# Attention with a learned position bias and a gated feed-forward block: bias stores moved from GpSimd's queue to SyncE's, one PSUM tile per half of a bias unit, and first attention steps placed between the last bias units

## The chip, the cores and the metric

The kernel runs on one core of a Trainium2 chip. The metric is the device time of one execution in microseconds (us); lower is better. The engines are TensorE (PE, its weight loads PEld), VectorE (DVE), ScalarE (ACT), GpSimd (POOL) and SyncE (SP), which issues most transfers. Each engine works through its own instructions in a fixed order.

## The reference, cut to what matters

Four batches, eight heads, 576 positions, head size 64. The bias added to the scores is a small two-layer network of the distance between two positions, divided by a factor of the row; it is the same for all batches. After the attention the eight heads are joined to 512 channels and a gated product of two linear layers (512 to 1536) goes through a third (1536 to 512).

```python
psi_rel = log1p(|i - j|);  psi_i = log1p(max(i, 1))
h = maximum((psi_rel / psi_i) * w1 + b1, 0)        # 32 hidden
scores = q @ k.T / 8 + (h @ w2)                    # bias per head
attn = softmax(scores) @ v                         # then heads joined: x
out = ((x @ w_a) * (x @ w_b)) @ w_out
```

## The kernel before, in words

**The bias.** The 576 rows are cut into units of 16. For the row chunk that is done first (rows 0 to 255) there are 16 units. A unit takes four hidden blocks of 128 partitions (`bias_relu`, L152: a scale and relu of a row of logarithms, on DVE at L160 or on ACT at L164; `nact` says how many go to ACT), four groups of matmuls with `w2` into PSUM (`bias_mm`, L168, L170), and one or two scaled copies from PSUM to an SBUF row `bo` on ACT (L186, and L189, which reads backwards and so mirrors the row). Units 0 to 3 are wider than 512 columns and are done in two halves; units 4 to 15 in one piece. A transfer then stores `bo` to the DRAM tensor `bias_d` (L191), from POOL's queue for these 16 units. In `first_units` the PSUM tile is `[128, 2, 512]`, one per unit, from two pools in turn (`two`, L923); both halves of a unit lie in one tile. `keep(n)` issues n matmuls on a block of ones whose result nobody reads (L897).

**The attention of the first batch.** `attn_steps` yields twice per tile of 128 rows; tile n needs its bias rows, loaded from `bias_d` on SP (`load_bias`, L480), its scores (`qk_pair`, L526, two heads at once), a sum with row minimum on DVE (`soft1`, L540), an exponential on ACT (L545), a normalisation (`soft2`, POOL and DVE, L590 to L596), a transpose on PE (`turn`, L608) with a copy on ACT, and the product with v (`pv_first`, L557). Tiles 0 to 7 need rows 0 to 127, so units 0 to 7 of the bias; tiles 8 to 15 need units 8 to 15.

**The feed-forward weights** come as 64-bit numbers in chunks of 512 KB (`w_load`, L275) and are converted on ACT and DVE (`w_unit`, L281 to L287, then `wab_parts`), one chunk per step of `wab_steps`. `fetch_to(3)` loads the first three chunks in its first step. `v_scale` (L226) takes the largest magnitude of v with four ACT passes (L237) and a small matmul.

**The order.** PE's order is the program's (`manual_schedule`); on the other engines a scheduler places the instructions, and `issue_after`, `paced` and `late` add orders: a load under `paced` stands behind the last entry of `rows_in` on SP's queue, work under `late` behind the last entries of `ttrs`, `exps`, `evs` and `pns` on its engine. In the head of the kernel (L926 to L940) `merge` interleaves generators: units 0 to 7 with the loads of q, k and v (`first_loads`), the first weight step, bias loads 0 to 5, then units 8 to 15 with `v_scale` and two weight steps, eight `keep` matmuls, and then the attention steps with weight steps between.

## Time and profile before

| | |
|---|---|
| median of three runs | 748.81 us |
| the runs | 749.63, 744.23, 748.81 us |
| the profiled execution | 744.93 us |
| its span | 743.1 us |
| PE, DVE, ACT, POOL busy | 94%, 68%, 59%, 39% |
| mean granted clock of TensorE | 0.988 |

The span reaches from the first to the last instruction; 1.8 us of the profiled execution lie outside it. A busy share is an average over stages: the change touches the first 40 us or so, where PE is far from full, and the rest has to be read as what follows from them.

### The profile page before, as it was taken

The numbers are of one execution on the slowest core, as the hardware profiler recorded it, in microseconds if no ns is written. First come the engines' busy times: TensorE is split into PE (matmuls) and PEld (weight loads), VectorE is DVE, ScalarE is ACT, GpSimd is POOL, SyncE is SP. The second block draws the span as 40 slices with busy tenths as digits, with TensorE's granted clock in tenths as the row PEclk, the third lists the DMA queues.
The fourth block names the chain that finished last, engine by engine and source line by source line (L and its number), as shares of the span: only waits on it lengthen the run. The fifth ranks groups of instructions, "written<-read, shape, count | busy, mean of one in ns | idle before, by whom it ended". The sixth has DMA issues, their size and how long they took to land.

```text
span 743.1 us, 15586 instructions
## 1 busy us (share of the span) xinstructions
PE 695.8 (94%) x5463; PEld 531.0 (71%) x5463; DVE 506.9 (68%) x1234; ACT 436.2 (59%) x957; POOL 291.0 (39%) x429
## 2 busy tenths in 40 slices
PE   6887899899899999999899799999999999999997
PEld 1255466688686565677687688888788888888886
DVE  7788799989964776666888879888987780211100
ACT  6867787878966687744565555565655653322310
POOL 3544423336762142333454335535553563311200
PEclk9999999999999999999899999999999999999999
DMA  8899776687744987999999999999999973000001
GB/s 249 298 390 305 239 238 215 203 286 247 239 135 129 226 214 145 211 207 199 272 224 260 242 265 252 235 239 259 244 275 249 223 132 112 2 10 21 1 15 43
DMA packets 178163, 147.69 MB, mean 199 GB/s; under 512 B 125092, under 2 KB 138148, under 8 KB 178084
## 3 DMA queue, kind: packets, MB, share of 16 engines
q1 hardware_dynamic: 170928, 130.92, 69.6%
q10 hardware_dynamic: 5876, 10.93, 5.2%
q0 software_dynamic: 1280, 4.84, 1.8%
q8 instruction: 43, 0.70, 0.4%
q14 instruction: 36, 0.29, 0.1%
HBM read 101.15 MB, written 17.18 MB: 159 GB/s over the span
## 4 chain that ended last, share of the span: by engine, by line
PE 52%; DVE 12%; issue 11%; POOL 9%; DMA 8%; ACT 6%; SPq 1%; POOLq 0%; ACTq 0%; DVEq 0%
PE ab L770 22%; PE o L814 15%; PE pv L636 5%; PE qk L512 4%; POOL ph L575 4%; PE psta L170 3%; DMA pt<-ph 3%; DVE p L540 2%; POOL sm L590 2%; POOL gl L790 2%; DMA wraw<-wb 2%; ACT p L545 2%; DMA bias<-bias_d 1%; DVE ks L417 1%; DVE ph L578 1%
## 5 line engine op out<-in xcount | busy, mean ns | idle before, releaser
L770 PEld LDWEIGHTS <-w16t 128*128 128x128 f16 x2592 | 248.2, 98 | 45.2 <-issue 13.1
L770 PE MATMUL ab<-x,w16t 128*128 128x256 f16 x2304 | 271.9, 274 | 0.9 <-DVE x L651 0.9
L545 ACT ACTIVATE p<-p,mn 128x576 f32<-128x576 f32 x144 | 111.7, 776 | 82.3 <-DVE mn L540 70.8
L578 DVE SCALAR_TENSOR_TENSOR ph<-p,sm,ph 128x64 f16<-128x64 f32 x192 | 108.5, 605 | 23.0 <-POOL ph L575 22.6
L540 DVE CUSTOM_DVE_ANT_0 p<-qk,bias 128x576 f32<-128x576 f32 x143 | 106.5, 747 | 24.9 <-PE qk L512 12.9
L814 PE MATMUL o<-wos,gh 128*128 128x512 f32 x384 | 120.3, 394 | 0.0
L575 POOL TENSOR_SCALAR ph<-p,sm 128x576 f16<-128x576 f32 x96 | 71.5, 745 | 118.5 <-DVE sm L591 111.2
L590 POOL TENSOR_SCALAR sm<-sm 128x1 f32<-128x1 f32 x144 | 58.3, 405 | 140.4 <-ACT p L545 138.8
L790 POOL TENSOR_TENSOR gl<-g,gh 128x256 fp32r<-128x256 f32 x96 | 72.7, 757 | 88.1 <-ACT gh L789 88.0
L754 DVE SCALAR_TENSOR_TENSOR g<-ab,wv,asb 128x256 f32<-128x256 f32 x84 | 40.3, 480 | 80.9 <-ACT asb L778 79.6
L789 ACT CAST gh<-g 128x256 fp32r<-128x256 f32 x96 | 38.8, 404 | 76.3 <-DVE g L754 76.2
L814 PEld LDWEIGHTS o<-wos,gh 128*128 128x128 f32 x384 | 69.5, 188 | 16.0 <-issue 3.7
L512 PE MATMUL qk<-ks,qs 128*128 128x288 f32 x384 | 73.6, 313 | 5.6 <-DVE mn L540 3.8
L814 PE MATMUL o<-wos,gl 128*128 128x512 f32 x192 | 75.0, 391 | 0.0
L512 PEld LDWEIGHTS qk<-ks,qs 128*128 128x128 f32 x384 | 56.3, 190 | 15.9 <-DVE mn L540 5.4
L596 POOL TENSOR_SCALAR p<-p,sm 128x576 f32<-128x576 f32 x48 | 48.0, 1000 | 31.4 <-DVE sm L591 25.9
L778 ACT ACTIVATE asb<-ab,wv 128x256 f32<-128x256 f32 x84 | 39.4, 469 | 28.9 <-PE ab L770 26.0
L636 PE MATMUL pv<-pt,vs 128*64 128x320 f16 (+1 forms) x560 | 43.2, 308 | 9.3 <-DMA pt<-ph 9.3
L636 PEld LDWEIGHTS <-vs 128*64 128x64 f16 x560 | 32.0, 114 | 21.9 <-issue 9.3
L608 PE MATMUL tp<-idn,p 128*128 128x128 f32 x240 | 36.6, 285 | 6.2 <-ACT ptf L613 6.2
L814 PEld LDWEIGHTS o<-wos,gl 128*128 128x128 f32 x192 | 36.0, 188 | 7.8
L821 ACT COPY osb<-o 128x512 f32<-128x512 f32 x18 | 10.5, 582 | 52.5 <-PE o L814 36.6
(105 smaller groups left out, 913.5 us busy)
## 6 DMA issues: line engine op xcount, KB each, us to landing
bias<-bias_d SPq DMA_DIRECT2D x127, 288.0 KB, 3.8
rv<-vd SPq DMA_DIRECT2D x32, 320.0 KB, 4.3
rk<-kd SPq DMA_DIRECT2D x24, 288.0 KB, 3.6
wraw<-wa SPq DMA_DIRECT2D x12, 512.0 KB, 6.6
wraw<-wb SPq DMA_DIRECT2D x12, 512.0 KB, 5.0
wraw<-wo SPq DMA_DIRECT2D x12, 512.0 KB, 4.1
bias_d<-bo ACTq DMA_DIRECT2D x20, 295.5 KB, 3.4
bias_d<-bo POOLq DMA_DIRECT2D x16, 295.5 KB, 7.6
```

Of the source, the lines that this page charges most:

```text
L512: nc.tensor.matmul(ps[:, hf, :HB], a, b[:, hf * HB:hf * HB + HB], start=(x == 0), stop=(x == len(prods) - 1))
L540: ttr = nc.vector.tensor_tensor_reduce(out=p.rearrange("p (a n) -> p a n", a=2), in0=ps[:, :, :HB], in1=bt.rearrange("p (a n) -> p a n", a=2),
L545: exps.append(nc.scalar.activation(p, p, AF.Exp, bias=mn, scale=-1.0, accum_out=sm))
L575: nc.gpsimd.tensor_scalar(out=ph[:, :S], in0=p, scalar1=rc, scalar2=1.0, op0=ALU.mult, op1=ALU.mult)
L578: ins = nc.vector.scalar_tensor_tensor(out=ph[:, o:o + c1 - c0], in0=p[:, c0:c1], scalar=rc, in1=ph[:, c0:c1], op0=ALU.mult, op1=ALU.subtract,
L590: nc.gpsimd.tensor_scalar(out=sm, in0=sm, scalar1=1e-9, scalar2=1.0 / (PS if u >= NF else 1.0), op0=ALU.add, op1=ALU.mult)
L596: nc.gpsimd.tensor_scalar(out=p, in0=p, scalar1=rc, scalar2=1.0, op0=ALU.mult, op1=ALU.mult)
L636: nc.tensor.matmul(ps[64 * j:64 * j + 64, o:o + N], v[:, j, :], p[:, j * N:j * N + N], start=(x == 0), stop=(x == len(prods) - 1),)
L754: nc.vector.scalar_tensor_tensor(out=g, in0=ab[:, 1], scalar=wv[:, f, 1:2], in1=asb, op0=ALU.mult, op1=ALU.mult)
L770: nc.tensor.matmul(ab[:, j], w16[nm, f][:, pw, kk, :], xs[px][:, kk, :], start=(x % (3 * KC) == 0), stop=(x % (3 * KC) == 3 * KC - 1),)
L790: nc.gpsimd.tensor_tensor(out=gl, in0=g, in1=gh.bitcast(F32), op=ALU.subtract)
L814: nc.tensor.matmul(o, g[:, sl], wos[f][:, p], start=(f == 0 and x == 0), stop=(f == FC - 1 and x == 2))
```

## The change

The stores of units 0 to 7 go on SP's queue, those of units 8 to 15 stay on POOL's. A store on SP is entered in `rows_in`, so that later paced loads stand behind it. All q and k loads are issued first, then units 0 to 7 with the first weight step (now two chunks) after unit 4, then bias loads 0 to 3, the v loads, and bias loads 4 and 5. Every half of a unit takes a PSUM tile of its own from a ring: four tiles for units 0 to 7, two (those that the attention's first scores don't use) for units 8 to 15. The last copy of a unit is entered in `evs`. Three attention steps stand between units 10 and 11, one between 13 and 14, and the copies of units 14 and 15 are ordered behind the last exponential. From unit 8 on, odd units have all four relus on DVE, and each unit has two `keep` matmuls; the block of eight is gone.

```diff
@@ bias_unit
-                nc.scalar.mul(ob[:, mid + c0:mid + e], ps[:, :e - c0], rl)
+                ev = nc.scalar.mul(ob[:, mid + c0:mid + e], ps[:, :e - c0], rl)
...
-        queue.dma_start(out=dst[:, :, :BW - 1], in_=ob[:, :BW - 1])
+        store = queue.dma_start(out=dst[:, :, :BW - 1], in_=ob[:, :BW - 1])
+        if queue is nc.sync:
+            rows_in.append(store)
+        return ev
@@ wab_steps
-        fetch_to(3)
+        fetch_to(2)
@@ first_units
-                hs = bias_relu(lambda g: h4[:, g], uls, un, int(un % 2 == 0 or un >= 8))
-                keep((10, 2, 2, 2, 1, 1, 1)[un] if un < 7 else 0)
-                bias_unit(bh, lambda: banks(un), un, hs, 6, nc.gpsimd)
+                hs = bias_relu(lambda g: h4[:, g], uls, un, int(un % 2 == 0))
+                keep((10, 2, 2, 2, 1, 1, 1)[un] if un < 7 else 2)
+                evs.append(bias_unit(bh, lambda: banks(un), un, hs, 6, nc.sync if un < NU0 // 2 else nc.gpsimd))
@@
-        def two(un):
-            return (qkp, eq)[un % 2].tile([128, 2, 512], F32, tag="qk", name="psta", bufs=1)
+        def banks(un):
+            ring = (0, 1, 2, 3) if un < NU0 // 2 else (2, 3)
+            i = ring[used[0] % len(ring)]
+            used[0] += 1
+            if i == 3:
+                return pvp.tile([128, 1, 512], F32, tag="pv", name="psta", bufs=1)
+            pool, tag = ((qkp, "qk"), (eq, "qk"), (tpp, "tp"))[i]
+            return pool.tile([128, 2, 512], F32, tag=tag, name="psta", bufs=1)[:, 0:1]
...
-            merge((units, NU0 // 2), (fl, 2 * NP))
-            next(wts)
-            for m in range(6):
+            for _ in range(NP):
+                next(fl)
+            for un in range(NU0 // 2):
+                next(units)
+                if un == 4:
+                    next(wts)
+            for m in range(4):
                 load_bias(m)
-            merge((units, NU0 // 2), (v_scale(0), 7), (wts, 2))
-        keep(8)
-        merge((asteps, 4), (wts, 1), ((keep(2) for _ in range(4)), 4))
-        merge((asteps, 2 * N0 - 10), (wts, 7))
+            run(fl)
+            for m in range(4, 6):
+                load_bias(m)
+            vs0 = v_scale(0)
+            merge((units, 3), (vs0, 5), (wts, 1))
+            for _ in range(3):
+                next(asteps)
+            merge((units, 3), (wts, 1))
+            next(asteps)
+            with tc.issue_after(exps[-1].ins):
+                run(units)
+        merge((asteps, 2), (wts, 1), ((keep(2) for _ in range(2)), 2))
+        next(vs0)
+        merge((asteps, 2), ((keep(2) for _ in range(2)), 2))
+        run(vs0)
+        merge((asteps, 2 * N0 - 14), (wts, 7))
```

## Rows read from the trace of the kernel before

**Rows 1.** The page: busy tenths of PE and DVE in 40 slices of the span.

```profile
PE   6887899899899999999899799999999999999997
...
DVE  7788799989964776666888879888987780211100
```

**Rows 2.** Windows: stretch, length; PE, PEld, DVE, ACT, POOL busy (count); clock, DMA, GB/s.

```profile
5.00:24.70 19.70, 13.66 (x114) 2.93 (x113) 17.45 (x46) 16.02 (x38) 8.19 (x7) 1.00 0.90 305
24.70:36.00 11.30, 9.45 (x77) 3.06 (x78) 6.41 (x23) 9.00 (x21) 6.86 (x9) 1.00 0.85 250
36.00:48.00 12.00, 9.05 (x51) 5.43 (x52) 9.11 (x24) 7.37 (x16) 5.20 (x10) 0.89 1.03 414
...
85.00:95.00 10.00, 8.60 (x64) 4.94 (x63) 5.77 (x19) 5.18 (x13) 2.89 (x5) 1.00 0.49 130
95.00:140.00 45.00, 42.23 (x343) 29.60 (x340) 44.34 (x113) 33.73 (x66) 14.47 (x21) 1.00 0.67 216
```

**Rows 3.** Timeline around the two halves of unit 0: start, us, engine, line, instruction.

```profile
5.62 1.54 PE L170 MATMUL psta<-w16t,w2s 128*32 128x288 f32 x8 [0.41 <-DVE w16t L160]
...
7.23 0.50 ACT L186 ACTIVATE bo<-psta,rls 128x288 f32<-128x288 f32 x1 [0.77 <-PE psta L170]
7.63 0.27 ACT L189 ACTIVATE bo<-psta,rls 128x15 f32<-128x15 f32 x1
...
7.94 0.16 PEld L170 LDWEIGHTS psta<-w16t,w2s 128*32 128x32 f32 x8 [1.32 <-ACT bo L189]
```

**Rows 4.** Groups by line, 4 to 24.7 us: busy us, mean ns, idle before, releaser.

```profile
L160 DVE TENSOR_SCALAR w16t<-u,lgs 128x560 f32<-128x560 f32 (+11 forms) x40 | 15.9, 472 | 2.2 <-PE psta L170 2.2
L170 PE MATMUL psta<-w16t,w2s 128*32 128x288 f32 (+8 forms) x104 | 11.3, 473 | 5.7 <-ACT bo L189 5.3 <-DVE w16t L160 0.4
...
L897 PE MATMUL pr<-w16t 128*128 128x512 f16 x14 | 4.8, 429 | 0.0
L237 ACT ACTIVATE junk<-rvf 128x640 f32<-128x640 f32 x4 | 2.9, 732 | 0.0
...
L170 PEld LDWEIGHTS psta<-w16t,w2s 128*32 128x32 f32 x104 | 2.3, 108 | 12.6 <-ACT bo L189 9.1 <-DVE w16t L160 2.3 <-issue 1.1
```

**Rows 5.** The same view, 24.7 to 36 us.

```profile
L170 PE MATMUL psta<-w16t,w2s 128*32 128x432 f32 (+6 forms) x56 | 6.0, 498 | 2.2 <-ACT bo L189 2.2
```

**Rows 6.** Timeline from the stores to the first attention tiles.

```profile
24.30 0.37 ACT L189 ACTIVATE bo<-psta,rls 128x127 f32<-128x127 f32 x1
...
24.97 0.99 POOL L191 DMA_DIRECT2D bias_d<-bo  x1 [0.59 <-ACT bo L189]
...
28.49 2.52 SPq L480 DMA_DIRECT2D bias<-bias_d  x5
...
35.99 0.76 DVE L540 CUSTOM_DVE_ANT_0 p<-qk,bias 128x576 f32<-128x576 f32 x1 [3.15 <-PE qk L526]
...
37.73 1.24 PE L526 MATMUL qk<-rkf,rqf 64*128 64x288 f32 x8
...
39.34 0.71 PE L608 MATMUL tp<-idn,p 128*128 128x128 f32 x5
```

**Rows 7.** Tile view of the store at 24.97 us: issue to landing.

```profile
DMA to landing us min/median/max: 3.4/3.4/3.4
```

**Rows 8.** DMA issues of the first 30 us: KB each, median us to landing.

```profile
bias_d<-bo POOLq DMA_DIRECT2D x11, 295.5 KB, 5.8
rvf<-vd SPq DMA_DIRECT2D x4, 320.0 KB, 5.1
...
bias<-bias_d SPq DMA_DIRECT2D x4, 288.0 KB, 7.1
wraw<-wa SPq DMA_DIRECT2D x2, 512.0 KB, 9.4
```

**Rows 9.** The page, DMA issues of the whole span: stores of the later units.

```profile
bias_d<-bo ACTq DMA_DIRECT2D x20, 295.5 KB, 3.4
```

**Rows 10.** Timeline: the chunk that the fourth weight step waits for.

```profile
43.34 0.67 ACT L281 ACTIVATE wt<-wraw 128x512 f32<-128x512 f32 x1 [0.59 <-DMA wraw<-wb]
```

More of the change, by code (lines that the diff above doesn't have):

```diff
@@ L185, in bias_unit @@
             if e > c0:
-                nc.scalar.mul(ob[:, mid + c0:mid + e], ps[:, :e - c0], rl)
+                ev = nc.scalar.mul(ob[:, mid + c0:mid + e], ps[:, :e - c0], rl)
             a, e = max(c0, 1), min(c1, mid + 1)
             if e > a:
-                nc.scalar.mul(ob[:, mid + 1 - e:mid + 1 - a], ps[:, a - c0:e - c0][:, ::-1], rl)
+                ev = nc.scalar.mul(ob[:, mid + 1 - e:mid + 1 - a], ps[:, a - c0:e - c0][:, ::-1], rl)
         dst = bias_d[:, un * UP:un * UP + 16 * RW].rearrange("h (r w) -> r h w", w=RW)
-        queue.dma_start(out=dst[:, :, :BW - 1], in_=ob[:, :BW - 1])
+        store = queue.dma_start(out=dst[:, :, :BW - 1], in_=ob[:, :BW - 1])
+        if queue is nc.sync:
+            rows_in.append(store)
+        return ev
     def bias_rows(h, i, n):
@@ L921, in first_loads @@
                 yield
-        def two(un):
-            return (qkp, eq)[un % 2].tile([128, 2, 512], F32, tag="qk", name="psta", bufs=1)
+        def banks(un):
[6 more added lines that the diff above has]
+            return pool.tile([128, 2, 512], F32, tag=tag, name="psta", bufs=1)[:, 0:1]
+        used = [0]
         fl = first_loads()
@@ L929, in attention_moe @@
         with tc.tile_pool(name="bh", bufs=1, side="right") as bh:
-            units = first_units(two)
-            merge((units, NU0 // 2), (fl, 2 * NP))
-            next(wts)
-            for m in range(6):
-                load_bias(m)
-            merge((units, NU0 // 2), (v_scale(0), 7), (wts, 2))
-        keep(8)
-        merge((asteps, 4), (wts, 1), ((keep(2) for _ in range(4)), 4))
-        merge((asteps, 2 * N0 - 10), (wts, 7))
+            units = first_units(banks)
+            for _ in range(NP):
[5 more added lines that the diff above has]
+            for m in range(4):
+                load_bias(m)
+            run(fl)
[14 more added lines that the diff above has]
+        merge((asteps, 2 * N0 - 14), (wts, 7))
         n0 = 2 * ends[0] - 2 * N0 + 6
```

## The prediction

> **What bounds the kernel now.** I read the page first. PE is at nine tenths or more in nearly all slices after the first eight, and DVE is nearly full in the first eight [rows 1]. So from about 150 us on PE sets the pace, and what comes before is a start-up in which no engine is always full. A saving in the first 40 us is worth what it moves forward the work behind it, and no more.
>
> The windows by stage came next [rows 2]. From 95 to 140 us DVE is busy 44.34 of 45 us: it converts weights and reduces scores, and that work is the same before and after. Ahead of it DVE has idle time: 2.25 us of 19.70 in the stage of the first eight units, 4.89 of 11.30 in the stage of the last eight, 2.89 of 12.00 in the stage of the first attention tiles, and 4.23 of 10.00 from 85 to 95 us. The change can only pay by taking some of the first three away, about 10 us together; the fourth lies behind it and I see nothing in the change that touches it. The DMA share is 1.03 with 414 GB/s from 36 to 48 us, so in that stage the transfers are full as well.
>
> Then I followed the start of the attention through the timeline. The copies of unit 7 start their last part at 24.30, its store leaves POOL at 24.97, five bias loads leave SP from 28.49, DVE reduces the first scores at 35.99, PE makes the second pair of scores at 37.73 and the first transpose at 39.34 [rows 6]. The bias loads go the moment that the last store has landed: it took 3.4 us [rows 7].
>
> Why is unit 7 finished only at 24.7? The timeline of unit 0 shows it: its second half goes into the other bank of the tile, and still its weight load stands until the mirrored copy of the first half (7.63 to 7.90) is done, at 7.94 [rows 3]. In all, PE's weight loads lost 9.1 us behind these copies up to 24.7, and the matmuls 5.3 us of it beyond the loads' cover [rows 4]; the last eight units lost 2.2 us more [rows 5]. PE, ACT and the copies take turns where they could overlap.
>
> **The first eight units.** With a tile for each half and four in the ring, PE need not wait for the copy just made. What is left on PE is its own work. The 104 matmuls to 24.7 us take 11.3 us; eight of them are unit 8's, some 1.0, which leaves 10.3. The fillers of units 1 to 7 are eleven at 0.30 (two take 0.6), 3.3 us; the ten in front run before the data is there [rows 4]. From 5.6 us, where the first bias matmul starts [rows 3], that is 19.2. DVE's 28 relus at 0.40 (15.9 by 40) take 11.2 us and end before 17 [rows 4], and ACT loses the four passes over v (2.9 us) out of this stage, so neither is later than PE. The copies of unit 7 add 0.9, as now from the end of its matmuls without a queue. Unit 7 is done at 20.1 instead of 24.7: 4.6 us earlier. The bound below is no gain, if ACT's order keeps the turns; the bound above is this sum, since PE's work is not shortened.
>
> **The stores on SP.** POOL's queue loses eight stores and SP's gains eight, behind twelve loads of q and k and around two weight chunks (1 MB). A store behind unit 4 waits on SP for that unit's copies, and so do the chunks behind it; these chunks are not used before the weight step among units 8 to 10, so nobody waits. The landing time on SP's queue is not shown for this stage. From below it is the 3.4 us of the stores that ACT issues later [rows 9] and of POOL's last [rows 7]; from above the 9.4 us of the chunks in the first 30 us, with POOL's median of 5.8 between [rows 8]. I take 4.5: v (1.28 MB) and one chunk are no longer in front, two chunks are. Then the bias loads leave at 20.2 + 4.5 = 24.7 instead of 28.49, 3.8 us earlier; by the two ends 4.9 earlier or 1.1 later.
>
> **From the bias loads to the second tiles.** The loads land in 7.1 us [rows 8], so the first scores are reduced at about 31.3 and 32.0, against 35.99 [rows 6], where they also waited 3.15 us for PE's scores; these now stand between units 10 and 11, done before the bias. PE's count to that point: units 8 to 13 are 1.0 plus five sevenths of 6.0 (5.3 in all) [rows 5], fillers 12 at 0.3 (3.6), one pair of scores 1.24, so 29.3 from 19.2; then it stands until DVE has read both tiles, makes the second pair from 32.1 to 33.3 (38.97 before, 5.6 earlier), then units 14 and 15 with their fillers (1.6 + 1.2), the next fillers, and the first transpose at about 36.7, 2.6 us before its 39.34. If the loads land in 5.1 us as those of v did [rows 8], PE is there 2 us sooner. So this point moves forward by 2.6 on PE and 5.6 on DVE, whose second pair of tiles is the next to start. Between the two I take 4.5, nearer to DVE, because DVE and not PE is short of time until 140 us and PE has 2.95 idle us from 36 to 48 to catch up [rows 2].
>
> **What the edits cost.** Four relus move from ACT to DVE, at most 0.47 each [rows 4], 1.9 us; they lie in the 4.89 us that DVE idles in the second half of the units [rows 2], and cost 1.9 if that idle time has been used up. The four passes over v (2.9 us, their read-outs apart) go from this early stage to the time after the v loads land; ACT is busy 9.00 of 11.30 there [rows 2], but loses four relus, so I take nothing, with 2 us as the upper end. The third and fourth chunk are now issued behind the bias loads, v and two more bias loads, near 28.5; they land in 9.4 us [rows 8] or more, at 38, and the third is wanted by ACT near 36. Before, the fourth came late instead: ACT stood 0.59 us for it at 43.34 [rows 10]. I take 0.5 us more than now, from -1 to +3. Sixteen fillers among the units replace eight behind them; they are counted above. The stores of units 8 to 15 stay on POOL, whose queue has eight fewer ahead. The entries in `evs` and `rows_in` issue nothing.
>
> The sum: 4.5 - 0.5 = 4.0 us. From 48 us on the order of work is unchanged, DVE is full from 95 to 140 us and PE afterwards, so nothing I see gives the gain back, and nothing adds to it. 744.93 - 4.0 = 740.9 us for the profiled execution, 0.54% less. That execution is 0.5% under the median of the three runs; on the median the same ratio gives 748.81 x 0.9946 = 744.8 us.
>
> **Rivals.**
>
> *Most of it is lost in SP's order.* The last three stores stand on one queue behind two weight chunks instead of on a queue of their own. At the 305 GB/s of this stage [rows 2] 1 MB is 3.4 us, and the second chunk is not through when store 7 is issued. If all of that is ahead of it, it lands after 7.9 us, the bias loads leave at 28.1, hardly before 28.49, and of the 4.0 us some 0.6 is left: 748.2. For it: the chunks took 9.4 us [rows 8]. Against it: some 4 us lie between the chunks' issue after unit 4 and the store of unit 7. The Trainium skill, "DMA: Bandwidth & Descriptors", section "Queues, rings and completion order", says that a DMA engine takes turns between queue rows packet by packet but uses up one row's ring in order; by that rule a store on POOL's row shared the engines with the loads and one on SP's row must wait for them, which speaks against this part of the change. No row here shows the order within a queue.
>
> *The transfers set the pace anyway.* From 36 to 48 us they are full [rows 2], and v comes later than now. If the tiles of that stage wait for bytes, an earlier start only waits longer: about 0, 748.8. Against it: DVE lost 2.89 us there and the named wait for a chunk is 0.59 [rows 10].
>
> *It pays twice.* If the bias loads land in 3.4 to 5 us and the third chunk comes in time, PE is at the first transpose 5 us sooner, and the 2.89 idle us of DVE from 36 to 48 go too: 8 to 9 us, 740.
>
> *Slower.* The passes over v stand in ACT's fixed order between the copies of units 8 to 10. Their loads stand on SP behind four bias loads (0.5 us each to issue), which stand behind store 7's landing. If it lands after 9.4 us, at 29.6, the bias loads leave until 31.6, v until 33.6, and v lands at 5.1 to 7.1 after that, near 40. ACT then holds the copies of units 9 to 15 and the first exponentials until 40, PE and POOL's stores stand with it, and the exponential of tile 1 is some 5 us later than now, with the next bias loads behind units 8 to 15 another 3: 748.8 + 8 = 757. It decides from about 34 us on: up to there v is earlier than the exponentials want ACT.
>
> **How the numbers follow.** The forecast, 2 to 7.5 us less, 0.53; little or nothing left (the first two rivals, 3 us less to 3 more) 0.20; twice, 0.19; slower 0.08. What this kernel's measurement can tell from no change is about 1%, 7.5 us: its three runs are 0.7% apart. Faster by more than that is the third case and the edge of the first, 0.22; slower is most of the last, 0.06; the rest 0.72. The range, 738.5 to 752, takes in the third case but for its edge and the second to its end.
>
> **What would show it.** Right: no weight load of a second half behind the copy of the first; unit 7's copies done near 20 us; its store landing in 3.4 to 6 us; the bias loads leaving near 25; the first reduction on DVE near 31; the full stretch of DVE that begins at 95 us starting 4 us earlier. Wrong: store 7 landing after 8 us; ACT standing for v or for the third chunk by several us; the same idle time of DVE in the first 48 us; or the lead there at 48 us and gone at 140.

## The result and the profile after

The change makes the kernel slower. Twenty runs of the kernel after have a median of 750.81 us (745.91 to 753.09), twenty of the kernel before on the same chip 745.14 us (739.01 to 749.63); the ratio is 1.0068, 95% interval 1.0044 to 1.0093. I had forecast 0.54% faster. The profiled execution after has a span of 749.7 us with a mean granted clock of 0.975, the one before 743.1 us with 0.988. In the kernel after, lines behind 190 or so stand three further down: the score reduction is L543, the passes over v are L240, the fillers L900.

The page first, the tenths of PE and DVE over the span, against [rows 1].

```profile
PE   9688899899899999999898999999999999999997
...
DVE  8649789979984676777798879887988781211100
```

DVE is fuller in the first slice (8 for 7) and emptier in the second and third (6 and 4 for 7 and 8). So the first units gained, and what follows them lost. The windows by stage say how much, column by column as in [rows 2].

```profile
5.00:24.70 19.70, 19.70 (x163) 5.37 (x165) 19.70 (x55) 15.17 (x35) 4.47 (x2) 1.00 0.77 243
24.70:36.00 11.30, 5.67 (x28) 2.08 (x28) 4.50 (x14) 5.14 (x12) 4.01 (x9) 0.68 0.96 305
36.00:48.00 12.00, 9.37 (x40) 3.11 (x41) 5.29 (x16) 7.65 (x18) 4.37 (x7) 0.64 0.91 353
85.00:95.00 10.00, 7.74 (x53) 4.65 (x52) 4.94 (x17) 5.16 (x12) 2.56 (x3) 0.76 0.43 132
95.00:140.00 45.00, 43.28 (x337) 28.86 (x334) 41.61 (x107) 30.33 (x60) 14.02 (x20) 0.98 0.67 218
```

In the first stage DVE has no idle time left (2.25 us before), while the transfers do less: 243 GB/s for 305. In the third stage DVE does 5.29 us of work in 12 (9.11 before), and TensorE's granted clock is 0.64, most of it at the lower level of 1.2 GHz. From 85 to 95 us the clock falls again, to 0.76 (1.00 before).

The half tiles do what the diff says. The timeline of unit 0 [rows 3] now has sixteen matmuls in one go, and the second half's weight load no longer stands behind the copy of the first:

```profile
5.37 1.94 PE L170 MATMUL psta<-w16t,w2s 128*32 128x288 f32 x16
...
6.90 0.50 ACT L186 ACTIVATE bo<-psta,rls 128x288 f32<-128x288 f32 x1 [0.77 <-PE psta L170]
...
18.14 0.36 ACT L189 ACTIVATE bo<-psta,rls 128x127 f32<-128x127 f32 x1
...
28.35 0.76 DVE L543 CUSTOM_DVE_ANT_0 p<-qk,bias 128x576 f32<-128x576 f32 x1 [2.71 <-DMA bias<-bias_d]
...
33.72 0.78 ACT L548 ACTIVATE p<-p,mn 128x576 f32<-128x576 f32 x1 [3.69 <-DVE mn L543]
...
33.73 2.28 PE L529 MATMUL qk<-rkf,rqf 64*128 64x288 f32 x6 [3.24 <-DVE mn L543]
...
37.78 0.74 ACT L240 ACTIVATE junk<-rvf 128x640 f32<-128x640 f32 x1 [2.17 <-DMA rvf<-vd]
...
40.24 0.76 ACT L548 ACTIVATE p<-p,mn 128x576 f32<-128x576 f32 x1
...
41.72 0.53 ACT L186 ACTIVATE bo<-psta,rls 128x352 f32<-128x352 f32 x1
42.15 0.44 ACT L189 ACTIVATE bo<-psta,rls 128x239 f32<-128x239 f32 x1
...
42.70 1.30 PE L611 MATMUL tp<-idn,p 128*128 128x128 f32 x5 [2.20 <-POOL p L599]
...
43.69 0.53 POOL L191 DMA_DIRECT2D bias_d<-bo  x1 [0.22 <-issue]
```

Unit 7's copies end at 18.50 instead of 24.67, and the first scores are reduced at 28.35 instead of 35.99 [rows 6]: a lead of 7.6 us. Then read on. ScalarE stands for v until 37.78; its four passes over v stand ahead of the third exponential (40.24) and of the copies of unit 14 (41.72). The first transpose on PE comes at 42.70, 3.4 us later than before [rows 6]. The row names POOL, but tile 0's probabilities were done near 35.2; what ends just ahead is the copy of unit 14 (42.15 + 0.44), and by the ring of the change the transposes take the PSUM bank that unit 14 used, so this copy is the likely cause. PE is slower too: from 29 to 39 us the granted clock is 0.50, and six score matmuls take 2.28 us where all eight took 1.24 before [rows 6]. The store of unit 15 leaves at 43.69. SP's queue shows both ends of it:

```profile
8.79 6.24 SPq L191 DMA_DIRECT2D bias_d<-bo  x5
...
17.20 1.83 SPq L191 DMA_DIRECT2D bias_d<-bo  x3
24.41 1.83 SPq L483 DMA_DIRECT2D bias<-bias_d  x4
26.28 4.38 SPq L225 DMA_DIRECT2D rvf<-vd  x4
...
38.66 10.31 SPq L483 DMA_DIRECT2D bias<-bias_d  x3
49.03 0.43 SPq L278 DMA_DIRECT2D wraw<-wb  x1
```

A length of 10.31 us for three loads is not work: they load rows that the last units store, so SP stands until the store of unit 15, which left at 43.69, has landed, and the weight chunks behind wait with it. Before, SP stood as well, in two places:

```profile
38.09 4.77 SPq L480 DMA_DIRECT2D bias<-bias_d  x2
...
46.65 7.24 SPq L480 DMA_DIRECT2D bias<-bias_d  x3
```

The second of these stands is 7.24 us long, and the transfers stay full through it (a share of 1.01), with loads on the way that SP issued from 42.96 to 45.7. In the kernel after, the last chunk issued ahead of the stand, at 37.77, lands 7.7 us later, and from 45 us on the share falls to 0.66 and then, up to 50, to 0.21. So a stand of SP need not cost transfers; this one does once what was issued ahead of it has landed. The chain of work that ended last names the two transfers that decide this stage, with start and length:

```profile
18.52 5.77 DMA bias_d<-bo
...
26.28 11.47 DMA rvf<-vd
```

How far ahead or behind the kernel is can be followed by the score reductions on DVE, one for each attention tile. These are their starts in us, read from the timeline of DVE, for the main kernels of this study:

| tile | before | after | v first | v first, units first | after, units first | before + 1 MB |
|---|---|---|---|---|---|---|
| 0 | 35.99 | 28.35 | 31.42 | 32.42 | 29.56 | 36.95 |
| 3 | 41.19 | 44.03 | 39.70 | 39.45 | 42.86 | 42.14 |
| 10 | 63.61 | 65.49 | 59.07 | 59.54 | 66.32 | 64.39 |
| 13 | 71.16 | 73.28 | 66.85 | 67.32 | 74.11 | 71.94 |
| 17 | 83.42 | 86.26 | 84.76 | 80.34 | 87.09 | 85.72 |
| 18 | 87.94 | 92.93 | 88.49 | 86.44 | 92.62 | 90.19 |
| 20 | 97.72 | 104.00 | 98.00 | 96.57 | 104.74 | 99.69 |
| 30 | 141.92 | 148.21 | 142.20 | 140.76 | 148.75 | 143.89 |

After, the lead of 7.6 us is a lag of 2.8 at tile 3 and 17 and of 6.3 at tile 20. From there on the two kernels run in step: the lag is 6.28 at tile 20 and 6.29 at tile 30, and the spans differ by 6.6. So between these two executions the whole result is made in the first 100 us, and tile 20 is the place at which to read the experiments. It is one execution of each kernel, though: the kernel with one MB more is the kernel before up to 53 us, and in its execution tile 0 comes 0.96 us later. Differences of a microsecond at one tile have to be taken with that in mind.

The windows also tell what has been moved by then. Before, then after, in four stretches up to 82.5 us:

```profile
0.00:25.00 25.00, 17.61 (x127) 4.38 (x131) 19.72 (x60) 17.61 (x39) 8.95 (x13) 1.00 0.84 276
25.00:42.50 17.50, 14.29 (x103) 5.37 (x96) 11.31 (x35) 12.08 (x29) 9.80 (x14) 1.00 0.92 314
42.50:50.00 7.50, 5.94 (x44) 4.24 (x40) 5.85 (x14) 5.41 (x12) 3.23 (x6) 0.77 1.04 413
50.00:82.50 32.50, 27.46 (x230) 17.36 (x226) 29.03 (x78) 25.65 (x56) 14.81 (x22) 1.00 0.97 330
```

```profile
0.00:25.00 25.00, 23.68 (x175) 6.80 (x175) 22.26 (x70) 17.04 (x37) 5.50 (x7) 1.00 0.73 226
25.00:42.50 17.50, 9.86 (x48) 2.67 (x40) 6.44 (x18) 9.50 (x24) 5.34 (x11) 0.71 1.01 351
42.50:50.00 7.50, 6.88 (x26) 3.52 (x26) 3.09 (x11) 3.04 (x8) 2.74 (x4) 0.54 0.62 217
50.00:82.50 32.50, 28.50 (x252) 18.68 (x251) 31.17 (x83) 27.84 (x60) 13.87 (x22) 1.00 1.00 353
```

GB/s by length gives 6.9, 5.5, 3.1 and 10.7 MB before, 26.2 in all, and 5.7, 6.1, 1.6 and 11.5 after, 24.9 in all. After, 1.2 MB are missing at 25 us, since v and a chunk are issued later than before, and 1.5 MB more in the 7.5 us up to 50, most of which SP stands. From 50 us on the transfers are full in both by their share (0.97 and 1.00), but a full share is no fixed rate: 330 GB/s before, 353 after.

### The profile page after: what moved, and what is told of

It reads as the page before. It is cut to its first block, busy times and chain, and to the rows that moved or that the text cites. A ratio compares the mean times of both kernels' runs of the same rounds, so it can differ in the third digit from the quotient of the medians.

```text
span 749.7 us, 15603 instructions
## 1 busy us (share of the span) xinstructions
PE 704.1 (94%) x5473; PEld 534.2 (71%) x5473; DVE 507.1 (68%) x1238; ACT 435.0 (58%) x953; POOL 281.7 (38%) x421
## 4 chain that ended last, share of the span: by engine, by line
PE 51%; DVE 13%; issue 11%; POOL 10%; DMA 8%; ACT 6%; SPq 1%; POOLq 0%; ACTq 0%; DVEq 0%
PE ab L773 20%; PE o L817 14%; PE pv L639 5%; POOL ph L578 3%; PE qk L515 3%; DMA pt<-ph 3%; PE psta L170 3%; DVE p L543 2%; POOL sm L593 2%; POOL gl L793 2%; PE pr L900 2%; DMA rvf<-vd 2%; ACT p L548 1%; PE tp L611 1%; DVE ph L581 1%
## 5 line engine op out<-in xcount | busy, mean ns | idle before, releaser
L543 DVE CUSTOM_DVE_ANT_0 p<-qk,bias 128x576 f32<-128x576 f32 x143 | 106.8, 747 | 33.7 <-DMA bias<-bias_d 11.9
L593 POOL TENSOR_SCALAR sm<-sm 128x1 f32<-128x1 f32 x144 | 56.3, 391 | 145.4 <-ACT p L548 143.6
L639 PE MATMUL pv<-pt,vs 128*64 128x320 f16 (+1 forms) x560 | 44.7, 316 | 10.5 <-DMA pt<-ph 10.2
L420 DVE TENSOR_TENSOR ks<-rk,ks 64x576 fp32r<-64x576 f32 x48 | 39.2, 816 | 2.0 <-ACT ks L423 0.5
```

Of the source, the lines that this page charges most:

```text
L543: ttr = nc.vector.tensor_tensor_reduce(out=p.rearrange("p (a n) -> p a n", a=2), in0=ps[:, :, :HB], in1=bt.rearrange("p (a n) -> p a n", a=2),
L593: nc.gpsimd.tensor_scalar(out=sm, in0=sm, scalar1=1e-9, scalar2=1.0 / (PS if u >= NF else 1.0), op0=ALU.add, op1=ALU.mult)
L639: nc.tensor.matmul(ps[64 * j:64 * j + 64, o:o + N], v[:, j, :], p[:, j * N:j * N + N], start=(x == 0), stop=(x == len(prods) - 1),)
```

## The experiments

Three theories, as the expectations name them. Theory 1 (also B, or order): v lands late and its passes, fixed in ScalarE's order, hold the third exponential and the copies of units 14 and 15, and what hangs on these. Theory 2 (also A, or bytes): the transfers are full up to some 85 us, so that the bytes moved set the time and an earlier first tile is only a longer wait. Theory 3: TensorE's order, with the second scores ahead of units 14 and 15, holds these units. Ratios are to the kernel before in the same set of runs.

**v loaded first.** The kernel after, with the v loads right behind q and k and the six bias loads together:

```
-            for _ in range(NP):
-                next(fl)
+            run(fl)
...
-            for m in range(4):
-                load_bias(m)
-            run(fl)
-            for m in range(4, 6):
+            for m in range(6):
                 load_bias(m)
```

> The changed kernel with the four v loads issued right behind the q and k loads, ahead of the first stores, so that the six bias loads follow each other. Theory 1 (late v: in the changed kernel v lands at 37.8 us, behind the bias loads, and its passes stand in ScalarE's fixed order ahead of the copies of units 14 and 15, so the stores of these and every load behind them on SyncE's queue come late): the passes run before 25 us without a wait, tile 3 is reduced before 39 us (44.0 in the changed kernel), the store of unit 15 leaves before 38 us (43.7), SyncE is free of it by 44 us (48.8), and the time is 6 to 11 us below the changed kernel, so at or below the kernel before. Theory 2 (bytes: the transfers of this stage are full whatever the order, an earlier start only waits longer): the 1.28 MB of v push the stores and the first reduction back by some 3 us, and the time is within 2 us of the changed kernel. Theory 3 (TensorE's order: the second pair of scores stands ahead of units 14 and 15 and waits for the second bias tile): unit 15 is still done near 39 us and the gain is under 5 us.

746.56 us, ratio 1.0034 (1.0002 to 1.0065). Tile 20 comes at 98.00: all of the 6.28 us but 0.28 is back. That the late v held this kernel, as theory 1 says, is so; its figures were too high: tile 3 comes at 39.70, the store of unit 15 leaves at 39.85, SP is free at 44.94, and the time is 4 us below the kernel after and not 6 to 11. Unit 15's matmuls end at 38.58, and the gain is under 5 us, as theory 3 gave, so TensorE's order may hold what is left. And it is back only to the level of before: a lead of 4.3 us at tile 13 is gone by tile 17. Its timeline on SP, PE and ScalarE, and two windows:

```profile
32.27 12.67 SPq L483 DMA_DIRECT2D bias<-bias_d  x3
...
38.95 0.71 PE L611 MATMUL tp<-idn,p 128*128 128x128 f32 x5
...
72.61 0.74 ACT L240 ACTIVATE rv<-rv 128x640 f32<-128x640 f32 x1 [3.15 <-DMA rv<-vd]
```

```profile
42.50:45.00 2.50, 2.44 (x18) 1.51 (x14) 1.35 (x6) 1.29 (x2) 0.75 (x1) 1.00 0.23 93
0.00:82.50 82.50, 67.97 (x497) 32.16 (x497) 65.16 (x187) 58.78 (x130) 27.55 (x45) 0.94 0.91 316
```

SP stands even longer, the transfers fall to a share of 0.23 meanwhile, and later ScalarE waits 3.15 us for v of the second batch.

**The passes over v behind units 14 and 15.** The kernel after with `vs0` taken out of the merge with the units and run behind them:

```
-            merge((units, 3), (vs0, 5), (wts, 1))
+            merge((units, 3), (wts, 1))
...
+            for _ in range(5):
+                next(vs0)
```

> The changed kernel with the four passes over v put behind units 14 and 15 in the program, the loads as they are. Theory 1: v lands as late as in the changed kernel, near 37.8 us, but the copies of units 14 and 15 no longer wait for it; the store of unit 15 leaves near 40 us instead of 43.7, SyncE is free near 45 instead of 48.8, and 3 to 6 us of the loss come back. Theory 2: within 1 us of the changed kernel. Theory 3: unit 15's matmuls end at 40 us as before, and the store leaves not before 40.5; 2 to 3 us come back.

749.99 us, 1.0080 (1.0047 to 1.0113): none of the 3 to 6 us that theory 1 gave come back in the total, and theory 2's "within 1 us" is what was measured. Tile 3 comes at 38.10, 5.9 us sooner, so the passes did hold it. Then the third chunk takes over, issued late on the same queue, with two of the passes behind it in ScalarE's order, in this kernel's table of waits:

```profile
PE pr L79 <- DVE vm L248: 10.0, 1, 10.0
...
ACT wt L284 <- DMA wraw<-wa: 5.3, 1, 5.3
```

PE stands 10.0 us for the maximum over v, ScalarE 5.3 for the third chunk, and tile 4 comes at 53.66 (49.96 after), tile 20 at 105.45. This order of the passes is no cure while the loads are late.

**The half tiles alone.** The kernel before with a ring of four half tiles, and all stores on POOL as they were:

```
-        def two(un):
-            return (qkp, eq)[un % 2].tile([128, 2, 512], F32, tag="qk", name="psta", bufs=1)
+        def banks(un):
+            ring = (0, 1, 2, 3) if un < NU0 // 2 else (2, 3)
...
-            units = first_units(two)
+            units = first_units(banks)
```

> The kernel before with nothing but the PSUM ring of the change (a tile for each half, four in turn for units 0 to 7, two for units 8 to 15); stores on GpSimd's queue, loads and attention as before. Theory 1 (the lead in the first 25 us is real and is lost only where v stands in the way): unit 7 is copied near 21 us instead of 24.7, the bias loads leave near 25 instead of 28.5, and 1 to 4 us are gained on the kernel before. Theory 2: the bias loads leave earlier and the time stays within 1 us of the kernel before.

745.41 us, 1.0035 (1.0007 to 1.0063). The first reduction comes at 39.18, 3.2 us later than before. So the gain that theory 1 gave did not come. The reason stands on POOL's row: the stores up to 23 us as a tile view (min, median and max in ns), the first of them, and DVE's last relus ahead of its first pause, then the same two for the kernel before:

```profile
L191 POOL DMA_DIRECT2D bias_d<-bo x6: 530/532/12042, 8.4 to 22.5; - x6
...
8.40 12.04 POOL L191 DMA_DIRECT2D bias_d<-bo  x1 [7.13 <-ACT bo L186]
...
16.76 3.56 DVE L160 TENSOR_SCALAR w16t<-u,lgs 128x448 f32<-128x448 f32 x10
```

```profile
9.59 4.22 POOL L191 DMA_DIRECT2D bias_d<-bo  x1 [8.33 <-ACT bo L186]
...
13.97 1.23 DVE L160 TENSOR_SCALAR w16t<-u,lgs 128x480 f32<-128x480 f32 x3 [0.27 <-PE psta L170]
```

It is one store that stands, not six: the first starts at 8.40 and ends at 20.44, 0.12 us after DVE's unbroken relus end (20.32), and the five behind it take 0.53 us each in DVE's pause. Before, DVE pauses at 13.70, and the first store, from 9.59, ends at 13.81. Some stores do get through beside relus (0.56 us at 19.78 before), and why is not shown. The Trainium skill says in "SBUF — State Buffer", section "Who interferes with whom", that a DMA which seems stalled by a DVE instruction is one that GpSimd has to prepare, and that the hardware queues don't suffer from it. The trace agrees: on SP's row after, stores take 0.6 us (1.83 by 3) beside a DVE that never pauses. With DVE kept busy without a pause, as the half tiles do, the stores have to leave POOL.

**All stores on POOL, with v first.** The kernel of the first experiment with the queue of the first eight stores set back:

```
-                evs.append(bias_unit(bh, lambda: banks(un), un, hs, 6, nc.sync if un < NU0 // 2 else nc.gpsimd))
+                evs.append(bias_unit(bh, lambda: banks(un), un, hs, 6, nc.gpsimd))
```

> The run with v first, with all stores on GpSimd's queue as in the kernel before. In the run with nothing but the half tiles six store instructions took GpSimd 14.7 us (8.4 to 23.1) beside DVE's unbroken relus, and unit 6 waited for them. If that comes from GpSimd beside a busy DVE, it comes again: the first six stores leave GpSimd after 20 us, unit 7 is copied after 24, the bias loads leave near 30 instead of 26.5, and the time is 2 to 5 us above the run with v first. If it came from the transfers of the stage, the stores leave as units are done and the time is within 1 us of the run with v first.

753.71 us, 1.0138 (1.0105 to 1.0171). Six stores take 15.37 us here, 12.74 of them the first, which ends 0.12 us after DVE's relus pause at 21.20; the bias loads leave at 31.84, and the kernel loses 1.0% against the one with v first. So the move to SP pays, given the half tiles.

**The stores on SP alone.** The kernel before with its first eight stores on SP (and their entries in `rows_in`), and nothing else:

```
-                bias_unit(bh, lambda: banks(un), un, hs, 6, nc.gpsimd)
+                bias_unit(bh, lambda: banks(un), un, hs, 6, nc.sync if un < NU0 // 2 else nc.gpsimd)
```

> The kernel before with nothing but the first eight stores on SyncE's queue (and later paced loads behind them). Unit 7 is done near 24.7 as before; its store lands in 3 to 6 us. Theory 1: the bias loads leave within 1 us of 28.5, v is early as before, and the time is within 1.5 us of the kernel before. Theory 2: the same. If the order on one queue costs much by itself (stores behind weight chunks), the bias loads leave after 30 and the time is 2 to 4 us above the kernel before.

753.99 us, 1.0127 (1.0091 to 1.0163). This tells little of the change: here the program's order puts a store between the loads of each head pair, so q, k and v wait for copies of units, and the first reduction is at 45.32. It shows the price of a store that stands ahead of loads on their queue.

**Weight chunks earlier.** Three kernels ask whether bytes moved early help: v first with six chunks right behind v, the kernel before with six chunks, and v first with its two chunks behind the bias loads. The first two edits turn on one line (the first from 2 to 6), the third on one step:

```
-        fetch_to(3)
+        fetch_to(6)
...
-                if un == 4:
-                    next(wts)
             for m in range(6):
                 load_bias(m)
+            next(wts)
```

> The run with v first, and now also the first six weight chunks (3 MB instead of two chunks after unit 4) issued behind v, ahead of every store. Theory A (bytes: every kernel so far had moved 27 MB at 88 to 90 us, with the transfers full from 25 to 85 us; a lead of the first tiles without bytes moved earlier is lost where the v loads of the next batch come late): about 9 MB moved at 25 us instead of 6.9, tile 0 is reduced no earlier than 31 us, perhaps 2 us later, but the 27 MB are through near 84 us, the lead of tile 13 (4.3 us on the kernel before) is still there at tile 20, and the time is 3 to 5 us below the run with v first and 1 to 4 below the kernel before. Theory B (only the waits in the order of SyncE and ScalarE cost): the stores stand behind 3 MB, tile 0 comes 3 us later, and the time is 1 to 3 us above the run with v first.

> The kernel before with six weight chunks fetched in the first step instead of three, nothing else. Theory A: 1.5 MB move into the gap of SyncE's queue from 13 to 28 us; tile 0 may come 1 us later, tile 20 comes 2 to 3 us earlier, and the time is 1 to 3 us below the kernel before. Theory B: within 1 us of the kernel before, or 1 above it.

> The run with v first, but the two weight chunks that stood between the stores of units 4 and 5 come behind the six bias loads. Theory A: stores land sooner, tile 0 is reduced 1 to 2 us earlier than the 31.4 of that run, 1 MB is moved later, and the time is 1 to 3 us above that run. Theory B: tile 0's lead lasts and the time is 0 to 2 us below that run.

749.06 us, 1.0073 (1.0044 to 1.0102); 746.01 us, 1.0030 (0.9999 to 1.0062); 747.24 us, 1.0039 (1.0009 to 1.0069). Theory 2's gain didn't come. In the first, tile 0 comes at 35.72, and 24.7 MB have moved at 82.5 us, less than in v first. With six chunks the kernel before has moved 9.3 MB at 30 us for 7.9, but 15.3 for 15.5 at 50 us and 26.1 for 26.2 at 82.5: the bytes won are lost in between. In the third the first reduction comes at 26.47, 9.5 us sooner than before, and at tile 17 (83.20) nothing of it is left. Then it loses 3.3 us more, where PE waits for the maximum over v of the second batch:

```profile
86.69 0.59 PE L79 MATMUL pr<-idn,vm 128*1 128x128 f32 x2 [3.14 <-DVE vm L248]
```

**The maximum of the second batch earlier.** Is it this maximum that takes the lead back? In three kernels it begins two tiles sooner:

```
-VS = N0 - 4, 2 * N0 - 4, 3 * N0 - 10
+VS = N0 - 6, 2 * N0 - 4, 3 * N0 - 10
```

> The kernel with the v loads first behind q and k (742.8 to 751.7 us, tile 13 reduced at 66.85 and tile 20 at 98.00), with one edit more: the maximum over the second batch's v begins two tiles sooner, so that its four loads and four ScalarE passes stand two tiles earlier in the order. Theory V (the lead of 4.3 us at tile 13 is lost because these loads take 7.6 us to land, ScalarE stands 3.15 us for the first, and TensorE's transposes stand behind the maximum): no wait for rv of a microsecond or more before tile 17, the maximum before 80 us instead of 85.44, tile 20 at 94 to 96 and the time 2 to 4 us under the same kernel without the edit. Theory A (the transfers, full from 50 to 75 us, bring what tile 20 needs at a fixed time): the wait moves to another load and tile 20 stays at 97 to 99, no gain. The steps behind tile 20 are also put in another order by the same edit, so the reduction of tile 20 is read first and the total second.

> The kernel before, with the maximum over the second batch's v begun two tiles sooner and nothing else, as the control for the run with v first. Before, ScalarE waits only 0.40 us twice for these loads. Theory V: the edit alone moves tile 20 by at most 1 to 2 us (97.72 before), since here that maximum isn't late. If it moves tile 20 by as much as in the other kernel, the gate is the maximum in both and the half tiles are not what pays. Theory A: no change.

> The kernel after, with the maximum over the second batch's v begun two tiles sooner and nothing else. After, TensorE stood 2.19 us behind that maximum at 89 us and its clock then fell to 0.53 of full in 90 to 95 us; tile 17 was 2.84 us behind the kernel before, tile 20 6.28. Theory V: the second half of the loss goes, tile 20 comes at 100 to 101 instead of 104.00, and the time is 3 us under after's; the first half (the first batch's v landing at 37.8) stays. Theory A: tile 20 stays at 104.

By their medians all three are slower than without the edit, though only the second beyond the intervals: 750.59 us, 1.0076 (1.0047 to 1.0106); 751.10 us, 1.0073 (1.0037 to 1.0109); 752.91 us, 1.0101 (1.0059 to 1.0142). Tile 20 comes at 108.83, 100.59 and 107.12, later by 10.8, 2.9 and 3.1 us. Theory V, as it is called there, falls. The maximum comes little sooner with v first (84.56 for 85.44) and clearly sooner in the others (78.81 for 83.30, 82.96 for 88.73), but PE's order now has it ahead of tile 16, and PE stands 2.50, 2.51 and 4.31 us for it. The other theory's "no change" didn't come either. So these runs don't say whether the maximum takes the lead: the edit moves PE's wait for it forward along with it.

**The last stores on ScalarE's queue.** v first, with the last eight stores moved:

```
-                evs.append(bias_unit(bh, lambda: banks(un), un, hs, 6, nc.sync if un < NU0 // 2 else nc.gpsimd))
+                evs.append(bias_unit(bh, lambda: banks(un), un, hs, 6, nc.sync if un < NU0 // 2 else nc.scalar))
```

> The kernel with v first, with the stores of units 8 to 15 on ScalarE's queue instead of GpSimd's. SP stood from 32.27 to 44.94 for the store of unit 15 in that kernel, with a transfer share of 0.64 in 40 to 45 us. Theory Q (GpSimd's queue, which starves beside DVE, delays that store): the last store lands some 2 to 4 us earlier, SP is free at 41 to 43, and tiles 8 to 13 come 1 to 3 us sooner; whether the total follows shows whether the loads behind that store decide it. Rival: the store waits for the copy of unit 15 in ScalarE's order and not for its queue, so SP is free at the same time, and each store costs ScalarE's order its issue.

743.96 us, 0.9980 (0.9954 to 1.0005). SP is free at 44.13 for 44.94, so the queue was little of it: the store waits for its unit. Tile 20 at 97.39, 0.61 us sooner than with POOL's queue; the ratio is 0.5% lower, in another set of runs, which so small a step doesn't explain.

**The units ahead of the scores.** This undoes the third part of the change, in the kernel just told, in the one with v first and in the kernel after:

```
-            merge((units, 3), (vs0, 5), (wts, 1))
-            for _ in range(3):
-                next(asteps)
-            merge((units, 3), (wts, 1))
-            next(asteps)
-            with tc.issue_after(exps[-1].ins):
-                run(units)
+            merge((units, NU0 // 2), (vs0, 5), (wts, 2))
+        for _ in range(4):
+            next(asteps)
```

> The kernel with v first and the last eight stores on ScalarE's queue (744.0 us; SP held from 33.85 to 44.13 behind the store of unit 15, 26.2 MB moved by 82.5 us), with units 8 to 15 all made ahead of the first attention tiles, as in the kernel before, and not around them. Theory bytes: the store of unit 15 goes at once, SP is held 4 to 7 us less, the transfer share of 0.35 in 42.5 to 45 us goes up to 0.9 or more, some 1 MB more has moved by 82.5 us, and tile 20 comes 2 to 3 us sooner (94.5 to 95.5 against 97.39); the time 741 to 742. Theory order: SP is free sooner, but tile 20 stays within a microsecond, since ScalarE's and TensorE's order decides.

> The kernel with v first and the last eight stores on GpSimd's queue (746.6 us; SP held from 32.27 to 44.94), with units 8 to 15 all made ahead of the first attention tiles. Theory bytes: the hole in the transfers at 42.5 to 47.5 us (shares 0.23 and 0.76) closes, tile 20 at 95 to 96 against 98.00, 2 us less time. Theory order: tile 20 within a microsecond of 98.00.

> The kernel after, with one part undone: units 8 to 15 all ahead of the first attention tiles and not around them; the v loads stay behind the first bias loads. Theory bytes: SP is free before 45 us instead of 49, the hole at 45 to 50 us (shares 0.66 and 0.21) closes, 1 MB more has moved by 82.5 us (24.9 after), and tile 20 comes at 100 to 101.5 instead of 104.00. Theory order (ScalarE's passes over the late v stand ahead of the copies, here of units 9 to 15): units 9 to 15 then wait for v until 38 us, and nothing or less is won.

743.16 us, 0.9992 (0.9969 to 1.0015); 741.19 us, 0.9974 (0.9945 to 1.0002); 752.05 us, 1.0109 (1.0087 to 1.0131). With v first on POOL's queue, the timeline on SP and PE, and three windows, become:

```profile
36.58 3.27 SPq L483 DMA_DIRECT2D bias<-bias_d  x3
...
83.11 0.38 PE L79 MATMUL pr<-idn,vm 128*1 128x128 f32 x2 [1.73 <-DVE vm L248]
```

```profile
0.00:82.50 82.50, 69.94 (x524) 33.33 (x524) 68.02 (x194) 62.01 (x135) 30.74 (x48) 0.96 0.94 325
...
42.50:50.00 7.50, 6.56 (x58) 4.37 (x54) 6.83 (x17) 5.24 (x11) 2.26 (x5) 1.00 1.04 411
...
85.00:90.00 5.00, 4.78 (x30) 3.19 (x29) 2.87 (x7) 3.00 (x6) 0.49 (x1) 0.66 0.21 59
```

The stand of 12.67 us is 3.27, the hole in the transfers is closed, 26.8 MB have moved by 82.5 us (26.1 with v first), and tile 20 comes 1.43 us sooner, at 96.57, short of the 2 to 3 that theory 2 gave. In the kernel with ScalarE's queue the hole closes as well, but tile 20 gains only 0.30 and the time nothing. In the kernel after the hole closes too (a share of 1.00 from 42.5 to 50 us), and 14.9 MB have moved at 50 us for 13.4, but undoing this part brings nothing: tile 20 comes 0.74 us later. v is late there all the same, and its passes now stand ahead of exponentials:

```profile
40.00 0.74 ACT L240 ACTIVATE junk<-rvf 128x640 f32<-128x640 f32 x1 [7.99 <-DMA rvf<-vd]
```

So the effect of this part depends on v, and a closed hole alone does not bring tile 20 forward. Tile 20, by the place of v and of the units:

| | units around the scores | units first |
|---|---|---|
| v behind the bias loads | 104.00 (after) | 104.74 |
| v first | 98.00 | 96.57 |

**One MB more.** The kernel before with two stores of 0.5 MB on SP's queue, of a constant tile to memory that nobody reads, behind bias loads:

```
+            if n in (8, 9):
+                with paced(): nc.sync.dma_start(out=ex_d[n - 8], in_=tab["idn"][:, None, :].broadcast_to([128, 8, 128]))
```

> The kernel before, with two stores of 0.5 MB each of a constant tile to memory that nobody reads, put on SP's queue among the bias loads of tiles 10 to 12, at about 50 to 56 us. Nothing waits for them. Theory bytes: 1 MB at about 400 GB/s is 2.5 us, and tile 20 comes 2 to 3 us later than 97.72 (and the time is 747 to 748). Theory order: the loads behind them have slack, tile 20 within 0.5 us.

747.78 us, 1.0045 (1.0018 to 1.0073); tile 20 at 99.69, 1.97 us later. But the stores left SP at 53.05 and 56.29, and this execution was behind already: by 0.96 us at tile 0 and by 0.78 at tiles 10 and 13. What the stores can have cost at tile 20 is 1.2 us, between the 2 to 3 of theory 2 and the 0.5 of theory 1; at the 337 GB/s of 50 to 82.5 us a megabyte takes about 3. So a megabyte that no instruction waits for costs something, by the total beyond the interval, and less than the time it takes to move. Two stores of few bytes, which would take SP's time alone, were not tried.

## Why the prediction was wrong

**Right: the first units.** Unit 7 done at 20.1 by the sum, 18.5 measured; its store landing in 4.5, 5.77 measured; the bias loads leaving at 24.7, 24.41 measured; the first reduction at 31.3, 28.35 measured. The good match of the third is luck: two misses of 1.6 and 1.3 us cancel. The fourth holds a slip (24.7 and 7.1 make 31.8) and a landing of 7.1 us where the first load was used 3.9 us after its issue. PE's waits behind the copies went as I had said, and the rival of a lost order on SP did not come: the bias loads left on time. Store 7 didn't test the order within SP's row, since the two chunks had landed by 19.8 and 22.0.

**The step that failed: v priced at nothing.** I wrote of the passes over v, "so I take nothing, with 2 us as the upper end", and took the landing of its loads, in the rival "Slower", at 5.1 to 7.1 us, a row of transfers early in the kernel [rows 8]. Issued behind four bias loads and with stores in flight, they took 11.47 us, the first landing at 37.76. ScalarE stood 2.17 us for it, three passes stood ahead of the third exponential (40.24, with its scores reduced by 36.6) and the fourth ahead of the copies of unit 14. The first transpose, which I put at 36.7, came at 42.70. Loading v first takes back 6.0 of 6.28 us at tile 20 of the profiled executions, and in the ratio of the medians half of the loss (1.0034 for 1.0068, with intervals that overlap from 1.0044 to 1.0065). So this step carries nearly all of the loss at tile 20; how much of the total's, the runs don't settle. The mechanism stood in my text as the rival "Slower", with the very point from which it decides, 34 us. I gave it 0.08 because I hung it on one cause, a late landing of store 7. The landing of v itself was the open price, and I had no row for it in full transfers, though the windows gave 1.03 for the stage in which it would land [rows 2].

**The path of the first transpose, mis-sized too.** With v first the first transpose comes at 38.95, 0.39 us sooner than before, where I had 2.6. I had counted PE's work at full clock; in that kernel the granted clock is 0.50 from 31 to 36 us, and the eight score matmuls of the second pair, begun at 32.24, end 3.05 us later, where I had 1.24; 0.8 us of it is a wait for the second tile's reduction.

**"Nothing I see gives the gain back".** This was wrong as well, since a lead of 4.3 us at tile 13 with v first is gone at tile 17; which term of mine hid it stays open. I had counted the last units behind the first scores on PE, 2.8 us of work, and not on SP, where three loads of bias rows stand for the store of unit 15: 10.31 us after, 12.67 with v first, 4.77 for the last two of them before. No chunk leaves meanwhile, and 1.5 MB less are moved from 42.5 to 50 us. That this hole costs time is not shown: undoing that part closes it in three kernels, and tile 20 comes 1.43 us sooner with v first, 0.30 sooner with the stores on ScalarE's queue as well, and 0.74 later in the kernel after.

**The rival I may have underrated: the transfers set the pace.** It was stated for 36 to 48 us and given a part of 0.20. There it doesn't hold: v first has moved 14.9 MB at 50 us, 0.6 less than before, and is 4.3 us ahead at tile 13. From there to tile 20 it fits: four kernels with v first (the first, the one with its chunks behind the bias loads, and the two with stores on ScalarE's queue) were 2.3 to 9.5 us ahead at tile 0 and had moved 26.0 to 26.2 MB by 82.5 us, for 26.2 before; at tile 20 none is more than 0.7 us ahead, and one is 3.3 behind. The one that had moved 26.8 is 1.15 ahead. But a kernel whose tiles are late also asks for its next loads late, so bytes and tiles go together whichever leads, and the one run that adds bytes alone gives 1.2 us for a megabyte. That the transfers take the lead is argued, not shown. What the runs do show is that no version tried is clearly ahead of the kernel before. The fastest version here, v first and the units ahead of the scores, has 0.9974 (0.9945 to 1.0002), and I can't call that a gain.

**Small terms.** The third chunk, taken at 0.5 us and to leave near 28.5, left at 35.32, but no wait in the kernel after can be put down to it: ScalarE converts it at 43.28 without standing, and DVE's wait of 2.03 us at 44.03, which the row gives to a chunk, ends with the first transposes (42.70 + 1.30), as the same reduction does with v first. The relus moved to DVE lie in its idle time, as I had said (4.50 us busy of 11.30 from 24.7 to 36).

**Open.** From tile 17 to 20 the best version loses 1.9 of its lead of 3.1 us. In that stretch PE stands 1.73 us for the maximum over v of the second batch, as much as in the kernel after, and its granted clock is 0.66 from 85 to 90 us where it was 1.00 before; in the kernel after it is 0.53 from 90 to 95. That the clock and that wait are the cause is argued, not shown; beginning the maximum sooner made it worse. The total of v first fell by 0.6% with the units ahead, in another set of runs, where tile 20 moved by 0.2%; what the rest is, the runs don't settle. The trace of that version is of the slowest of its twelve executions (746.39 us, median 741.19): there the lead of 1.16 us at tile 30 is lost behind it, and the span is 744.6 us for 743.1 before.

## What to carry to other kernels

Price a load by the row of a load in the state in which it will run: the same 320 KB landed in 5.1 us early and in 11.5 us behind full transfers, and ScalarE, whose order was fixed, passed that on to an exponential and to the copies of two units. When a step moves behind another, follow its store to the load that waits for it, and ask what stands on that load's queue and how much is still on its way: three waiting loads held SP for 10 us, and the transfers ran out for the last four of these. And before counting a lead, follow it to the point where it is to be spent: here leads of 2 to 9.5 us at the first tile were 1.2 us or less at tile 20.

## What the runs showed of the hardware that was not expected

Issuing a store from GpSimd took 0.53 us in a pause of DVE. One that began beside back-to-back relus on DVE stood for the whole row of them, 12.04 us with the half tiles alone, 12.74 in the kernel with all stores on POOL and v first, 4.22 before, and each ended 0.12 us after DVE's pause began. TensorE had work for 5.67 us of 11.30 from 24.7 to 36 in the kernel after, and its granted clock fell there to 0.50, its lower level; it was at that level again from 42.5 to 47.5 us, with PE busy 4.38 of 5. A transpose group of five then took 1.30 us for 0.71 at full clock [rows 6], so a wait of PE is followed by slower work.
